# The end of a fused decode layer: the last addition as an fp32 product, the output by halves from partitions 0 and 1

## Chip, cores and metric

One core of a Trainium2 chip. The metric is the device time of one execution in microseconds, median over runs on the chip; the profile is one such execution, and its span (first to last instruction) is about 1.8 us shorter than the device time. The runs were made in several calls on different chips, so each kernel is compared with the kernel before in its own call.

The views name the engines PE (TensorE, the matrix products; PEld loads its weights), DVE (VectorE), ACT (ScalarE), POOL (GpSimd) and SP (SyncE); SPq and ACTq are the instructions with which SP and ACT issue transfers. The granted clock is the share of TensorE's full clock that the throttle allows.

## The reference

Attention of one new token (batch 2, 32 query heads over 16 key heads, the last 2048 keys of a bf16 cache) and a squared-ReLU MLP read the same normalised `x`; their outputs are added:

```python
xn = _layernorm(x, axis=-1)          # x: (2, 1, 576)
return x + _A_ref(xn, k, v, wq, wo) + _B_ref(xn, w1, b1, w2, b2)
# _B_ref: h = xn @ w1 + b1; r = max(h, 0); out = (r * r) @ w2 + b2   (w2: 4608 x 576)
```

The output is 2 x 576 bf16. Some 53.6 MB are loaded for it.

## The kernel before

Everything accumulates in PSUM. `out_ps` takes x, b2, the attention's output and three quarters of the MLP; it holds columns 0 to 287 in partitions 0 and 1 and columns 288 to 575 in partitions 32 and 33. The last quarter of w2 is loaded in two pieces (rows 0 to 6 and 7 to 8 of each partition) and accumulates in `tail_ps`, four quarters of 144 columns in four column groups, so that its few products run together:

```python
def mlp_tail(r0, r1):
    w2_sb = w2_tiles.pop((NG4 - 1, r0))
    if r0 == 0:
        mlp["out"] = psum.tile([P, OQ], F32, tag="misc", name="tail_ps")   # OQ = 144
        nc.vector.memset(mlp["out"][:], 0.0)
    for r in range(r0, r1):
        o = (r - r0) * D
        for i in range(4):
            pe_mm(mlp["out"][32 * i:32 * i + B, :], lhsT=mlp["h"][:, (NG4 - 1) * FR + r, :],
                  rhs=w2_sb[:, o + i * OQ:o + (i + 1) * OQ], start=(r == 0), stop=(r == FR - 1),
                  skip_group_check=True, tile_position=(0, 32 * i))
# ... (cut)
for w in W2P[:NG4 - 1]:
    mlp_o(*w)                                  # three quarters into out_ps
for i in range(4):                             # copy the rest to where tail_ps has it
    cp = nc.scalar.copy if i % 2 else nc.vector.tensor_copy
    cp(out=part[32 * i:32 * i + B, :],
       in_=out_ps[32 * (i // 2):32 * (i // 2) + B, (i % 2) * OQ:(i % 2 + 1) * OQ])
for w in W2P[NG4 - 1:]:
    mlp_tail(*w[1:])
fin_sb = work.tile([RB, OQ], BF16, tag="fin", name="fin_sb")               # RB = 98
nc.vector.tensor_tensor(out=fin_sb[:], in0=mlp["out"][0:RB, :], in1=part[:], op=ALU.add)
for b, eng in ((0, nc.sync), (1, nc.scalar)):  # one output row on each queue
    eng.dma_start(out=out2d[b:b + 1, :].rearrange("o (q n) -> (o q) n", q=4), in_=fin_sb[b:RB:32, :])
```

Of the kernel before, what the change touches and what calls it, by code (L numbers as in the profile page):

```python
# [8 lines left out]
F32 = mybir.dt.float32  # L9
BF16 = mybir.dt.bfloat16  # L10
ACT = mybir.ActivationFunctionType
ALU = mybir.AluOpType
# [4 lines left out]
def kernel(  # L17
# [14 lines left out]
    nc = tc.nc  # L32
    P = 128
    B, Sq, D = A_x.shape
# [30 lines left out]
    NG4 = 4  # L65
# [6 lines left out]
    RB = 32 * (NG4 - 1) + B  # L72
    OH = D // 2
    OQ = D // 4
# [3 lines left out]

    const = ctx.enter_context(tc.tile_pool(name="const", bufs=1))
    kvpool = ctx.enter_context(tc.tile_pool(name="kvpool", bufs=6))  # L80
    ktpool = ctx.enter_context(tc.tile_pool(name="ktpool", bufs=3))
    wbig = ctx.enter_context(tc.tile_pool(name="wbig", bufs=NFULL // RW))
    wrem = ctx.enter_context(tc.tile_pool(name="wrem", bufs=1))
    wopool = ctx.enter_context(tc.tile_pool(name="wopool", bufs=1))
    work = ctx.enter_context(tc.tile_pool(name="work", bufs=2))
# [3 lines left out]
    def pe_mm(out, **kw):  # L89
        return tc.keep_in_program_order(nc.tensor.matmul(out, **kw))  # L90
# [5 lines left out]
    out2d = out.rearrange("b s d -> (b s) d")  # L96
# [62 lines left out]
    nc.scalar.dma_start(out=x_sb[:], in_=x2d)  # L159
    eps_t = const.tile([B, 1], F32, name="eps_t")  # L160
    nc.vector.memset(eps_t[:], 1e-5)
    warm = const.tile([B, 34], F32, name="warm")
    nc.scalar.activation(out=warm[:, 0:1], in_=eps_t[:], func=ACT.Sqrt)
    for f in issue_kv(k_tiles, A_k_cache, 0, "k"):
        f()
# [14 lines left out]
    ident_f = const.tile([P, P], F32, name="ident_f")  # L180
# [27 lines left out]
    for sg in range(S):  # L208
# [8 lines left out]
                            op=ALU.add)  # L217
# [6 lines left out]
                            in0=ident[0:TH, 0:TH].unsqueeze(1).unsqueeze(3).to_broadcast([TH, P // NC, TH, rep]),  # L224
# [3 lines left out]
                          in_=ident[0:TH, 0:TH].unsqueeze(1).to_broadcast([TH, NT * 32 // TH, TH]))  # L228
    par = const.tile([P, 2, 2, Dh // 2], BF16, name="par")
    for e in range(2):  # L230
        nc.gpsimd.tensor_copy(out=par[:, e, :, :],
                              in_=ident[:, e:Dh:2].unsqueeze(1).to_broadcast([P, 2, Dh // 2]))
# [7 lines left out]
    out_ps = psum.tile([32 + B, OH], F32, tag="out", name="out_ps")  # L240
    nc.vector.memset(out_ps[:], 0.0)

    def out_acc(lhsT, rhs_of, start=False, stop=False):
        for i in range(2):
            pe_mm(out_ps[32 * i:32 * i + B, :], lhsT=lhsT, rhs=rhs_of(i * OH, (i + 1) * OH),
                  start=start, stop=stop, skip_group_check=True)
# [152 lines left out]
    mlp = {}  # L399
# [30 lines left out]
    def mlp_o(g, r0, r1):  # L430
        w2_sb = w2_tiles.pop((g, r0))
        for r in range(r0, r1):
            o = (r - r0) * D
            out_acc(mlp["h"][:, g * FR + r, :], lambda a, z: w2_sb[:, o + a:o + z], stop=(g == NG4 - 2 and r == r1 - 1))

    part = const.tile([RB, OQ], F32, name="part")
    nc.gpsimd.memset(part[:], 0.0)

    def mlp_tail(r0, r1):
        w2_sb = w2_tiles.pop((NG4 - 1, r0))  # L440
        if r0 == 0:
            mlp["out"] = psum.tile([P, OQ], F32, tag="misc", name="tail_ps")
            nc.vector.memset(mlp["out"][:], 0.0)
        for r in range(r0, r1):
            o = (r - r0) * D
            for i in range(4):
# [3 lines that stand above are left out]
# [9 lines left out]
    W2P = [(0, 0, 9), (1, 0, 9), (2, 0, 9), (3, 0, 7), (3, 7, 9)]  # L459
# [36 lines left out]
    for w in range(2):  # L496
# [7 lines left out]
                          in_=ident[0:NG4, 0:NG4].unsqueeze(2).to_broadcast([NG4, NG4, 32]))  # L504
# [34 lines left out]
    wo_acc(1)  # L539
    for w in W2P[:NG4 - 1]:  # L540
        mlp_o(*w)
    for i in range(4):
        cp = nc.scalar.copy if i % 2 else nc.vector.tensor_copy
        cp(out=part[32 * i:32 * i + B, :],  # L544
           in_=out_ps[32 * (i // 2):32 * (i // 2) + B, (i % 2) * OQ:(i % 2 + 1) * OQ])
    for w in W2P[NG4 - 1:]:
        mlp_tail(*w[1:])

    fin_sb = work.tile([RB, OQ], BF16, tag="fin", name="fin_sb")
    nc.vector.tensor_tensor(out=fin_sb[:], in0=mlp["out"][0:RB, :], in1=part[:], op=ALU.add)  # L550
    for b, eng in ((0, nc.sync), (1, nc.scalar)):
        eng.dma_start(out=out2d[b:b + 1, :].rearrange("o (q n) -> (o q) n", q=4), in_=fin_sb[b:RB:32, :])


# [28 lines left out]
```

## Time and profile before

| | before |
|---|---|
| device time, median of 6 (range) | 134.69 us (134.63 to 134.99) |
| span of the profiled run | 132.7 us |
| queue of the loads | 53.61 MB, 95.0% of the span |
| last landing of w2 to the end | 3.55 us |

The prediction shows the lines behind this table. Loads run from the first slices to 129.2 us without a gap. Whatever is done before that is hidden; only the 3.55 us after the last landing can be shortened or lengthened by this change, unless it disturbs the loads (the prediction's rival D).

### The profile page before, as it was taken

Reading aid. Unit: us, or ns where it says so; the run is one execution under the profiler, and the core shown is the slowest. Engines: PE = TensorE matmul, PEld = TensorE weight load, DVE = VectorE, ACT = ScalarE, POOL = GpSimd, SP = SyncE. Lnnn points to the kernel's source line nnn. Section 1 sums busy time; section 2 is a strip of 40 time slices with the busy share of each in tenths; the row PEclk is TensorE's granted clock in tenths of the full one; section 3 lists DMA queues with packets and bytes.
Section 4 is the critical chain, followed back from the end, with each engine's and each line's share of the span. In section 5 each row is a group of like instructions: output and inputs, shape, how many; then the busy total and the mean of one; then the engine's idle time right before and its main releaser. Section 6 shows DMA issues by size and latency. Waiting matters only on the chain.

```text
span 132.7 us, 2060 instructions
## 1 busy us (share of the span) xinstructions
PE 92.7 (70%) x838; PEld 55.9 (42%) x838; DVE 61.2 (46%) x169; ACT 46.3 (35%) x63; POOL 7.5 (6%) x21
## 2 busy tenths in 40 slices
PE   0069456897499689688787629959937985556960
PEld 0058222673456355444444325524515942313640
DVE  6914304346533872863764772287041436443010
ACT  5717301494343274175175043412040661000010
POOL 7500000100100100100100100010000001000000
PEclk9999977779769999999999995995995599655896
DMA  4999999999999999999999999999999999999940
GB/s 159 396 412 449 415 444 415 439 420 430 437 420 444 415 449 415 439 425 434 425 415 449 420 435 433 427 433 444 417 425 430 430 434 439 406 425 434 414 203 1
DMA packets 4268, 53.74 MB, mean 405 GB/s; under 512 B 542, under 2 KB 544, under 8 KB 1060
## 3 DMA queue, kind: packets, MB, share of 16 engines
q1 hardware_dynamic: 4184, 53.61, 95.0%
q8 instruction: 6, 0.10, 0.3%
q0 software_dynamic: 64, 0.01, 0.0%
q14 instruction: 2, 0.02, 0.0%
q10 hardware_dynamic: 12, 0.00, 0.0%
HBM read 53.62 MB, written 0.00 MB: 404 GB/s over the span
## 4 chain that ended last, share of the span: by engine, by line
DMA 88%; PE 7%; SPq 3%; issue 0%; DVE 0%; DVEq 0%
DMA k<-in_A_k_cache_dram 67%; DMA w<-in_B_w_dram 21%; PE kT_ps L93 4%; SPq L111 1%; PE pv_ps L90 1%; SPq L118 1%; PE sc_ps L90 1%; SPq L123 0%; PE tail_ps L90 0%; DVE fin_sb L550 0%; PE sm L90 0%; DVEq L550 0%
## 5 line engine op out<-in xcount | busy, mean ns | idle before, releaser
L93 PE MATMUL kT_ps<-ident_f,k 128*128 128x128 f32 x256 | 43.7, 322 | 6.6 <-DMA k<-in_A_k_cache_dram 4.9
L297 ACT COPY kT<-kT_ps 128x1024 bf16<-128x1024 bf16 x32 | 31.8, 1012 | 30.1 <-PE kT_ps L93 30.1
L93 PEld LDWEIGHTS kT_ps<-ident_f,k 128*128 128x128 f32 x256 | 34.3, 165 | 18.6 <-issue 6.6
L299 DVE COPY kT<-kT_ps 128x1024 bf16<-128x1024 bf16 x32 | 22.0, 686 | 29.9 <-PE kT_ps L93 29.1
L90 PE MATMUL sc_ps<-kT,qz 128*32 128x512 bf16 x128 | 9.7, 383 | 6.2 <-DVE kT L299 5.5
L90 PE MATMUL pv_ps<-v,pT 128*32 128x512 bf16 x128 | 13.5, 467 | 0.0
L330 ACT ACTIVATE pr<-sc_ps,nb 128x512 bf16<-128x512 f32 x8 | 5.5, 687 | 20.7 <-DVE nb L327 20.7
L323 POOL PARTITION_ALL_REDUCE gmax<-m x8 | 2.9, 364 | 102.7 <-DVE m L321 80.4
L368 DVE SCALAR_TENSOR_TENSOR acc<-pv_ps,f,acc 128x128 f32<-128x128 f32 x24 | 8.3, 346 | 0.5
L90 PE MATMUL sm<-acc,tohead 128*64 128x128 f32 x16 | 4.2, 352 | 5.8 <-DVE acc L368 5.5
L332 DVE STREAM_TRANSPOSE pT<-pr 128x512 bf16<-128x512 bf16 x8 | 5.7, 709 | 5.2 <-ACT pr L330 5.2
L90 PE MATMUL out_ps<-wo,ws 128*2 128x288 bf16 x64 | 6.7, 390 | 1.1 <-DVE ws L390 1.1
L319 DVE TENSOR_REDUCE mx<-sc_ps 128x1 f32<-128x512 f32 x8 | 5.5, 692 | 3.4 <-PE sc_ps L90 3.0
L90 PEld LDWEIGHTS <-qz 128*32 128x32 bf16 x128 | 2.0, 94 | 10.0 <-DVE kT L299 7.1
L544 ACT COPY part<-out_ps 2x144 f32<-2x144 f32 x2 | 0.5, 268 | 15.0 <-DVE part L544 14.9
L90 PEld LDWEIGHTS <-ws 128*2 128x2 bf16 x64 | 3.7, 114 | 4.6 <-DVE ws L390 1.5
L90 PE MATMUL sm<-sums,samec 128*128 128x1 f32 x16 | 3.3, 276 | 3.1 <-DVE od L386 3.1
L90 PEld LDWEIGHTS sm<-acc,tohead 128*64 128x64 f32 x16 | 1.8, 161 | 8.6 <-DVE acc L368 7.9
L90 PEld LDWEIGHTS <-xnT 128*2 128x2 bf16 x100 | 2.6, 87 | 6.7 <-issue 5.5
L90 PEld LDWEIGHTS <-pT 128*32 128x32 bf16 x128 | 3.3, 102 | 4.3 <-issue 4.0
L90 PE MATMUL q_ps<-wq,xnT 128*2 128x512 bf16 x32 | 2.9, 499 | 3.2 <-DMA wq<-in_A_wq_dram 3.2
L93 PE MATMUL pro_ps<-ident,xn_sb 2*128 2x2 bf16 x4 | 0.3, 172 | 6.7 <-DVE xn_sb L198 6.7
(86 smaller groups left out, 62.3 us busy)
## 6 DMA issues: line engine op xcount, KB each, us to landing
k<-in_A_k_cache_dram SPq DMA_DIRECT2D x8, 2048.0 KB, 22.0
v<-in_A_v_cache_dram SPq DMA_DIRECT2D x8, 2048.0 KB, 27.0
wo<-in_A_wo_dram SPq DMA_DIRECT2D x2, 2304.0 KB, 23.4
w<-in_B_w_dram SPq DMA_DIRECT2D x2, 2304.0 KB, 30.9
wq<-in_A_wq_dram SPq DMA_DIRECT2D x2, 2048.0 KB, 13.9
w<-in_B_w_dram SPq DMA_DIRECT2D x3, 1296.0 KB, 27.7
w<-in_B_w_dram SPq DMA_DIRECT2D x1, 1008.0 KB, 31.8
w_rem<-in_B_w_dram SPq DMA_DIRECT2D x1, 576.0 KB, 34.2
```

The lines of the kernel that those rows point to most:

```text
L90: return tc.keep_in_program_order(nc.tensor.matmul(out, **kw))
L93: return tc.keep_in_program_order(nc.tensor.transpose(**kw))
L111: return [lambda i=i: nc.sync.dma_start(out=tl[:, i * n:(i + 1) * n], in_=v[:, :, i * n:(i + 1) * n]) for i in range(parts)]
L118: nc.sync.dma_start(out=tl[:, 0:RW * width], in_=rows[:, i * RW * width:(i + 1) * RW * width])
L297: nc.scalar.copy(out=dst, in_=src)
L299: nc.vector.tensor_copy(out=dst, in_=src)
L319: nc.vector.tensor_reduce(out=mx[:], in_=sc_ps, axis=AX.X, op=ALU.max)
L323: nc.gpsimd.partition_all_reduce(gmax[:], m2[:], channels=P, reduce_op=ReduceOp.max)
L330: nc.scalar.activation(out=pr[:], in_=sc_ps, func=ACT.Exp, bias=nb[:], scale=scale, accum_out=sums[:])
L332: nc.vector.transpose(out=pT[:].rearrange("p t m -> p (t m)"), in_=pr[:])
L368: op = nc.vector.scalar_tensor_tensor(out=nx[:], in0=pv_ps[:, j, :], scalar=f[:, j:j + 1], in1=acc[:], op0=ALU.mult, op1=ALU.add)
L544: cp(out=part[32 * i:32 * i + B, :], in_=out_ps[32 * (i // 2):32 * (i // 2) + B, (i % 2) * OQ:(i % 2 + 1) * OQ])
```

## The change

Its intent: add the rest not by a DVE addition over 98 partitions, but inside the accumulators, by a product with an identity; then the accumulators are copied to two partitions and leave as two halves of 576 B a row. Core of the diff:

```diff
-    ktpool = ctx.enter_context(tc.tile_pool(name="ktpool", bufs=3))
+    ktpool = ctx.enter_context(tc.tile_pool(name="ktpool", bufs=2))
-    warm = const.tile([B, 34], F32, name="warm")
+    warm = const.tile([B, 114], F32, name="warm")
-    part = const.tile([RB, OQ], F32, name="part")      # and its memset, and that of tail_ps
+    part = const.tile([B, D], F32, name="part")
 ...
-    for i in range(4):                                 # four copies to four quarters
-        ...
-    for w in W2P[NG4 - 1:]:
-        mlp_tail(*w[1:])
+    for i in range(2):
+        nc.vector.tensor_copy(out=part[:, i * OH:(i + 1) * OH], in_=out_ps[32 * i:32 * i + B, :])
+    mlp_tail(*W2P[NG4 - 1][1:])
+    for i in range(4):
+        pe_mm(mlp["out"][32 * i:32 * i + B, :], lhsT=ident_f[0:B, 0:B], rhs=part[:, i * OQ:(i + 1) * OQ],
+              start=False, stop=False, skip_group_check=True, tile_position=(0, 32 * i))
+    mlp_tail(*W2P[NG4][1:])
-    nc.vector.tensor_tensor(out=fin_sb[:], in0=mlp["out"][0:RB, :], in1=part[:], op=ALU.add)
-    for b, eng in ((0, nc.sync), (1, nc.scalar)):
-        eng.dma_start(out=out2d[b:b + 1, :].rearrange("o (q n) -> (o q) n", q=4), in_=fin_sb[b:RB:32, :])
+    for i, (cp, eng) in enumerate(((nc.vector.tensor_copy, nc.sync), (nc.scalar.copy, nc.scalar))):
+        fin_sb = work.tile([B, OH], BF16, tag="fin", name=f"fin_sb_{i}")
+        for q in range(2):
+            k = 2 * i + q
+            cp(out=fin_sb[:, q * OQ:(q + 1) * OQ], in_=mlp["out"][32 * k:32 * k + B, :])
+        eng.dma_start(out=out2d[:, i * OH:(i + 1) * OH], in_=fin_sb[:])
```

More of the change, by code (lines that the diff above doesn't have):

```diff
@@ L434, in mlp_o @@
             out_acc(mlp["h"][:, g * FR + r, :], lambda a, z: w2_sb[:, o + a:o + z], stop=(g == NG4 - 2 and r == r1 - 1))
-    part = const.tile([RB, OQ], F32, name="part")
-    nc.gpsimd.memset(part[:], 0.0)
+    part = const.tile([B, D], F32, name="part")
     def mlp_tail(r0, r1):
@@ L442, in mlp_tail @@
             mlp["out"] = psum.tile([P, OQ], F32, tag="misc", name="tail_ps")
-            nc.vector.memset(mlp["out"][:], 0.0)
         for r in range(r0, r1):
@@ L541 @@
         mlp_o(*w)
+    for i in range(2):
+        nc.vector.tensor_copy(out=part[:, i * OH:(i + 1) * OH], in_=out_ps[32 * i:32 * i + B, :])
+    mlp_tail(*W2P[NG4 - 1][1:])
     for i in range(4):
-        cp = nc.scalar.copy if i % 2 else nc.vector.tensor_copy
-        cp(out=part[32 * i:32 * i + B, :],
-           in_=out_ps[32 * (i // 2):32 * (i // 2) + B, (i % 2) * OQ:(i % 2 + 1) * OQ])
-    for w in W2P[NG4 - 1:]:
-        mlp_tail(*w[1:])
-    fin_sb = work.tile([RB, OQ], BF16, tag="fin", name="fin_sb")
-    nc.vector.tensor_tensor(out=fin_sb[:], in0=mlp["out"][0:RB, :], in1=part[:], op=ALU.add)
-    for b, eng in ((0, nc.sync), (1, nc.scalar)):
-        eng.dma_start(out=out2d[b:b + 1, :].rearrange("o (q n) -> (o q) n", q=4), in_=fin_sb[b:RB:32, :])
+        pe_mm(mlp["out"][32 * i:32 * i + B, :], lhsT=ident_f[0:B, 0:B], rhs=part[:, i * OQ:(i + 1) * OQ],
[7 more added lines that the diff above has]
+        eng.dma_start(out=out2d[:, i * OH:(i + 1) * OH], in_=fin_sb[:])
 _INS = ['A_x', 'A_k_cache', 'A_v_cache', 'A_wq', 'A_wo', 'B_x', 'B_w1', 'B_b1', 'B_w2', 'B_b2']
```

## The prediction

> **What bounds the kernel now.** I read the page first (engines' shares, the 40 slices, queues, the chain that ended last), then the chain piece by piece, then the timeline of the last microseconds. From the page:
>
> ```profile
> DMA  4999999999999999999999999999999999999940
> q1 hardware_dynamic: 4184, 53.61, 95.0%
> DMA 88%; PE 7%; SPq 3%; issue 0%; DVE 0%; DVEq 0%
> DMA k<-in_A_k_cache_dram 67%; DMA w<-in_B_w_dram 21%; PE kT_ps L93 4%; SPq L111 1%; PE pv_ps L90 1%; SPq L118 1%; PE sc_ps L90 1%; SPq L123 0%; PE tail_ps L90 0%; DVE fin_sb L550 0%; PE sm L90 0%; DVEq L550 0%
> ```
>
> The DMA row is full from the second slice to the next to last, and one queue moves 53.61 MB in 95% of the span of 132.7 us. So the loads set the time, and compute counts only after the last load has landed. The pieces of the chain at its end (start, length, what):
>
> ```profile
> 101.64 27.55 DMA w<-in_B_w_dram
> ...
> 129.23 0.32 PE tail_ps L90 x8
> ...
> 129.65 0.31 DVE fin_sb L550
> ```
>
> The last rows of w2 land at 129.19. Eight products take 0.32 us, a semaphore some 0.1, the DVE addition 0.31, and from 129.98 the output transfers run to the end, 2.72 us for issue, write and closing. The diff touches this tail almost alone. Its timeline:
>
> ```profile
> 127.66 0.63 DVE L544 COPY part<-out_ps 2x144 f32<-2x144 f32 x2 [7.07 <-PE out_ps L90]
> 128.04 0.56 ACT L544 COPY part<-out_ps 2x144 f32<-2x144 f32 x2 [14.94 <-DVE part L544]
> ...
> 128.52 1.00 PE L90 MATMUL tail_ps<-w,hT_sb 128*2 128x144 bf16 x36 [0.90 <-DMA w<-in_B_w_dram]
> ...
> 129.65 0.31 DVE L550 TENSOR_TENSOR fin_sb<-tail_ps,part 98x144 bf16<-98x144 f32 x1 [1.36 <-PE tail_ps L90]
> 129.98 0.66 SPq L552 DMA_DIRECT2D out_dram<-fin_sb  x1
> ```
>
> Two loads end the stream: rows 0 to 6 of the last w2 quarter (1008 KB) release TensorE at 128.52, rows 7 and 8 (288 KB) at 129.23, 0.71 us later. Narrower cuts of the timeline show that the 28 products of the first load started between 128.52 and 128.90 in groups of four, about 0.06 us apart (0.38 us over 27 gaps is 14 ns each), so TensorE has free time only from about 128.96 to 129.23: **0.27 us**.
>
> **What the skill says.** (1) FP8 and Floating Point Precision, section TensorE Precision Notes: true fp32 takes four passes through the array. The trace agrees in the one fp32 product of this shape: eight calls gave 16 instructions, and two of them started about 0.13 us apart at full clock for 128 columns (0.40 us for both less 0.27 for one), close to two passes of 128 columns each.
>
> ```profile
> 46.24 0.40 PE L90 MATMUL sm<-acc,tohead 128*64 128x128 f32 x2 [0.41 <-DVE acc L368]
> 32.78 0.28 PE L90 MATMUL out_ps<-x_sb,ident 2*2 2x288 bf16 x2
> ```
>
> (2) TensorE: Matmul & The Clock Gate, Part 3, "What overlaps and what doesn't": products start and end in program order, while those in different column groups may run at once. The trace agrees: 14 ns from start to start in the tail is a quarter of the 0.06 us of one group, and the two products of the second line above took 0.28 us together, as long as one alone (median 0.278). (3) TensorEngine Tiling (Array Packing), Key Properties: a change of tiling mode drains the array. The trace is compatible: the last score product ahead of that second line started at 32.48; products of that row follow each other in one group after about 0.23 us (32.24 to 32.47), yet the 2-row products came at 32.78, about 0.07 to 0.09 us later than that. (4) DMA: Bandwidth & Descriptors, Specifications: under 512 B a transfer pays a read-modify-write. The output now goes as four pieces of 288 B per queue and would go as two of 576 B. The trace does not show such a cost by itself: the write lies inside the 2.72 us.
>
> **The change part by part.**
>
> *Removed, no gain.* The GpSimd memset of `part` (0.22 us at 1.6 us) and the DVE memset of `tail_ps` (0.18 us at 118.9) lie beside other work. Both go, worth 0.
>
> *Two instead of three kT tiles.* Each half unit of K fills one tile. When the copies for the first half of unit u+1 want a buffer again, its reader, the first scores of unit u, stands ahead of unit u+1's transposes on the in-order TensorE, and the copies wait for these anyway. The same holds for the second half. No new wait: 0. I take the smaller pool to be room for the wider `part`, which goes from 576 to 2304 B per partition; with `warm` (136 to 456 B) the constants grow by 1728 + 320 = 2048 B, so the big load tiles keep their position modulo 2 KiB. I expect the rate of about 430 GB/s in the middle slices to stay.
>
> *Copies of the rest.* Two DVE copies of 2x288 replace four of 2x144. A 2x144 copy takes 0.298 us; at about 1.04 ns a column (the DVE copies of 128x512 fp32 in the transposed-reduction row take 0.69 us, which gives about the same slope) a 2x288 one takes about 0.45. From 127.66 that ends near 128.6. The fp32 products come no earlier than 128.96, so there are 0.35 us in hand: 0.
>
> *The fp32 products.* Four calls are eight instructions of two passes of 144 columns each: 288 columns at the measured 0.06 us per 144 give 0.12 us an instruction. The two halves of one call use one column group, so the second starts 0.12 after the first. Only the first half of the next call can start with it, because of program order. The starts are at 0, .12, .12, .24, .24, .36, .36 and .48, with the end of streaming at 0.60. Beginning at 128.96 without any drain, the last eight bf16 products then end about 0.35 us later than now (final group start 129.64 against 129.29). If the change from 128-row to 2-row operands and back drains the array, 0.08 to 0.09 us is added twice: 0.53. I take **+0.44**. The free 0.27 us is already deducted in both.
>
> *The end.* One DVE addition of 0.31 us becomes two DVE copies of 2x144 one behind the other. The like pair at 127.66 took 0.63, so **+0.32**. ACT's pair took 0.56 and runs beside it: at line 544 an ACT copy of one quarter (128.04) ran during a DVE copy of another (127.98), and here the engines read different quarters of the partitions again. The DVE pair and the SP queue's issue (0.66 against ACT's 0.61) set the end.
>
> *Output.* Same two issues, half the pieces, each twice as long: **-0.05**, a guess about a part that the trace does not separate.
>
> Sum: 0.44 + 0.32 - 0.05 = +0.71 us. On 134.68 that is 135.39; I put down 135.35, because the later launch of work might also hide a little.
>
> **Rivals.**
>
> *A: the fp32 products are hidden.* If their passes interleave over the four groups, they need some 0.24 us and fit the 0.27 us nearly whole. Against it: the instructions of one call stand together and start in order. The sum would be +0.16 or less for TensorE, about 135.0 in all.
>
> *B: they run one after another.* If fp32 takes the whole array, eight times 0.12 is 0.96 us, which with drains makes TensorE's part about +0.9 and the time 135.9. The bf16 2-row pair at 32.78 that ran together speaks against it, but no fp32 product in column groups is in this trace.
>
> *C: the output write becomes cheaper than I think,* as the diff's intent seems to be (rows of 576 B from partitions 0 and 1). If the 288 B pieces cost a few tenths, the end gives back 0.2 to 0.4 and the time is about 135.0. With A it would be near 134.7, no change.
>
> *D: the moved buffers alter the load stream.* Every load tile changes its address. One per cent of DMA rate is 1.3 us, more than all the rest together. For it: the loads are the bound. Against it: the padding keeps the alignment, and order, sizes and queue of the loads stay.
>
> *E: ACT waits for DVE at the end,* if the reads of the shared accumulator are put in order: ACT's pair would end 0.56 us later still, 135.9. The overlap at line 544 speaks against it.
>
> **Range and chances.** A and C give the lower part, B and E the upper; D widens both sides. I take 134.75 to 135.9. Two per cent is 2.7 us, far beyond any sum of these terms, so the chance of "within 2%" is 0.97, with 0.01 for faster and 0.02 for slower (D or a stall that I don't see).
>
> **What would show it right or wrong.** In the changed profile the DMA row and the landing of the last w2 rows should stay within about 0.3 us of 129.2. TensorE should have 846 products instead of 838. The last `tail_ps` products should end some 0.35 to 0.55 us after where they end now (129.53), not 0.1 (A) nor 0.9 (B). Two DVE copies of about 0.3 us each should stand in a row ahead of the SP issue, with ACT's beside them. From SP's issue to the end there should be 2.6 to 2.75 us; clearly less is C. If the last load lands much earlier or later, D holds and my sum says nothing about the time. Last, no copy of kT should wait longer than before for a buffer.

## The result, and the profile after

| | before | after |
|---|---|---|
| device time, median of 6 (range) | 134.69 us (134.63 to 134.99) | 134.51 us (134.37 to 134.59) |
| ratio | | 0.998 (95%: 0.9967 to 0.9993) |
| span of the profiled run | 132.7 us | 132.7 us |

A ratio is the mean time of one kernel's runs over that of the other's of the same rounds, so not quite the ratio of the medians quoted. The result lies within 2%, as forecast, but below the stated range of 134.75 to 135.9, on the other side of "before".

The page of the kernel after: the loads are as they were.

```profile
DMA  4999999999999999999999999999999999999950
q1 hardware_dynamic: 4180, 53.61, 95.1%
```

The timeline of its tail (start, length, engine, what, count, and in brackets the idle time before it with what ended it):

```profile
127.50 0.93 DVE L541 COPY part<-out_ps 2x288 f32<-2x288 f32 x2 [8.86 <-PE out_ps L90]
...
128.64 0.61 PE L90 MATMUL tail_ps<-w,hT_sb 128*2 128x144 bf16 x28 [1.17 <-DMA w<-in_B_w_dram]
...
129.17 0.42 PE L90 MATMUL tail_ps<-part,ident_f 2*2 2x144 f32 x8
...
129.53 0.29 PE L90 MATMUL tail_ps<-w,hT_sb 128*2 128x144 bf16 x8
129.85 0.63 DVE L552 CAST fin_sb<-tail_ps 2x144 bf16<-2x144 f32 x2 [1.42 <-PE tail_ps L90]
129.92 0.57 ACT L552 CAST fin_sb<-tail_ps 2x144 bf16<-2x144 f32 x2 [17.45 <-PE tail_ps L90]
130.50 0.33 SPq L553 DMA_DIRECT2D out_dram<-fin_sb  x1
```

The eight fp32 instructions are there, the two pairs of copies run side by side, and the issue at the end takes 0.33 us where it took 0.66. To add this up, both tails are put on one zero: the last landing of w2, which the trace's semaphore records give. Output packets are from the trace's packet records. All in us after that landing:

| kernel, clock in the tail | landing at | last 8 products start | their end | copies or addition start | SP issue starts | first SP output packet | end |
|---|---|---|---|---|---|---|---|
| before, full | 129.19 | 0.04 | 0.34 | 0.46 | 0.80 | 2.15 | 3.55 |
| after, full | 129.30 | 0.22 | 0.52 | 0.55 | 1.20 | 2.00 | 3.42 |

Step by step: the fp32 products delay the last eight by 0.18; the gap from the products' end to the first DVE instruction shrinks from 0.12 to 0.03 (-0.09; the addition had a further wait instruction ahead of it, probably since it needed `part` as well); two copies in place of one addition take 0.32 longer; from issue to end there are 2.22 us in place of 2.76 (-0.54; the prediction's 2.72 came from the rounded span). The sum is -0.13, close to the -0.18 of the medians. That the two spans are equal to a tenth is because the loads of this one profile landed 0.12 us later (over all twenty profiles the last landing lies between 129.11 and 129.48).

### The profile page after: what moved, and what is told of

The parts are those of the page before. It is cut to its first block, busy times and chain, and to the rows that moved or that the text cites. A ratio compares the mean times of both kernels' runs of the same rounds, so it can differ in the third digit from the quotient of the medians.

```text
span 132.7 us, 2075 instructions
## 1 busy us (share of the span) xinstructions
PE 90.6 (68%) x846; PEld 54.2 (41%) x846; DVE 61.5 (46%) x169; ACT 46.2 (35%) x63; POOL 7.3 (6%) x20
## 4 chain that ended last, share of the span: by engine, by line
DMA 73%; PE 13%; SPq 4%; DVE 3%; issue 2%; ACT 2%; POOL 1%; ACTq 0%; POOLq 0%
DMA w_rem<-in_B_w_dram 26%; DMA w<-in_B_w_dram 24%; DMA k<-in_A_k_cache_dram 23%; PE kT_ps L93 8%; PE pv_ps L90 2%; PE sc_ps L90 2%; SPq L118 1%; ACT kT L297 1%; SPq L111 1%; DVE kT L299 1%; DVE mx L319 1%; PE tail_ps L90 1%; POOL gmax L323 1%; SPq L142 0%; SPq L123 0%
## 5 line engine op out<-in xcount | busy, mean ns | idle before, releaser
L93 PEld LDWEIGHTS kT_ps<-ident_f,k 128*128 128x128 f32 x256 | 33.4, 163 | 20.2 <-issue 7.6
L90 PE MATMUL sc_ps<-kT,qz 128*32 128x512 bf16 x128 | 10.5, 413 | 6.5 <-DVE kT L299 5.5
L90 PE MATMUL pv_ps<-v,pT 128*32 128x512 bf16 x128 | 12.4, 428 | 0.0
L90 PE MATMUL sm<-acc,tohead 128*64 128x128 f32 x16 | 3.7, 315 | 5.7 <-DVE acc L368 5.5
L319 DVE TENSOR_REDUCE mx<-sc_ps 128x1 f32<-128x512 f32 x8 | 5.5, 691 | 4.2 <-PE sc_ps L90 3.8
L90 PE MATMUL out_ps<-wo,ws 128*2 128x288 bf16 x64 | 5.9, 356 | 1.1 <-DVE ws L390 1.1
L552 ACT CAST fin_sb<-tail_ps 2x144 bf16<-2x144 f32 x2 | 0.5, 272 | 17.5 <-PE tail_ps L90 17.4
L541 DVE COPY part<-out_ps 2x288 f32<-2x288 f32 x2 | 0.9, 448 | 8.9 <-PE out_ps L90 8.9
```

Source lines behind the costliest of these rows:

```text
L90: return tc.keep_in_program_order(nc.tensor.matmul(out, **kw))
L93: return tc.keep_in_program_order(nc.tensor.transpose(**kw))
L319: nc.vector.tensor_reduce(out=mx[:], in_=sc_ps, axis=AX.X, op=ALU.max)
L541: nc.vector.tensor_copy(out=part[:, i * OH:(i + 1) * OH], in_=out_ps[32 * i:32 * i + B, :])
```

## The experiments

### What in the output transfer cost: pieces, their size, or the source

The largest miss is the output, so it came first. The output leaves in pieces, each one row of the source tile that is contiguous on both sides. Theory P says that issue and set-up grow with the number of pieces, theory Z that pieces under 512 B are slow, theory S that a source is slow which takes every 32nd partition. The first two kernels change only the pieces, by a gap in the SBUF tile:

```diff
-        fin_sb = work.tile([B, OH], BF16, ...)
+        fin_sb = work.tile([B, 2, OQ + 16], BF16, ...)
-            cp(out=fin_sb[:, q * OQ:(q + 1) * OQ], ...)
+            cp(out=fin_sb[:, q, 0:OQ], ...)
-        eng.dma_start(out=out2d[:, i * OH:(i + 1) * OH], in_=fin_sb[:])
+        eng.dma_start(out=out2d[:, i * OH:(i + 1) * OH].rearrange("b (q n) -> b q n", q=2), in_=fin_sb[:, :, 0:OQ])
```

(Four pieces of 288 B; the second kernel does the same with four gaps of 72 columns, eight pieces of 144 B.)

> The changed kernel, but each output transfer goes as four pieces of 288 B (two partitions, two pieces each, kept apart by a gap in the SBUF tile) in place of two of 576 B. Theory P (issue and set-up grow with the number of pieces): SP issue back to 0.6 to 0.66 us, from issue start to first output packet about 1.35 us as before the change, time 0.4 to 0.55 us above the changed kernel, so 0.25 to 0.35 above the kernel before. Theory S (it was the step of 32 partitions at the source that cost): issue 0.33, time as the changed kernel. Theory Z (pieces under 512 B are written slower): issue 0.33, but packets or landing later by 0.1 to 0.5 us.

> As the run with four pieces, but eight of 144 B per transfer. P: SP issue 1.2 to 1.3 us, first packet some 2.4 us after issue start, time about 1.5 us above the changed kernel. S: as the changed kernel. Z: issue 0.33 us, landing later.

Measured: 135.05 us (134.4 to 135.34; before 134.87; ratio to before 1.0005, 0.9985 to 1.0024) and 134.76 us (ratio 0.9983, 0.9971 to 0.9996). The output's instructions with four pieces, with shortest, median and longest duration in ns:

```profile
L553 SPq DMA_DIRECT2D out_dram<-fin_sb x1: 327/327/327, 131.3 to 131.3; - x1
```

With eight pieces SP's issue took 326 ns. The first SP packet came 0.75 us after the start of the issue in both. So theory P is refuted. From the end of the last output packet to the last landing it took 0.44 and 0.43 us (after: 0.46), so theory Z is refuted as well. The longer times of the four-piece kernel have another cause, at least in its profiled run, treated below: the tail ran at half clock.

The third kernel goes the other way, one piece of 1152 B on each queue:

```diff
-        eng.dma_start(out=out2d[:, i * OH:(i + 1) * OH], in_=fin_sb[:])
+    for b, eng in ((0, nc.sync), (1, nc.scalar)):        # one tile [2, 576] written by DVE and ACT
+        eng.dma_start(out=out2d[b:b + 1, :], in_=fin_sb[b:b + 1, :])
```

> The changed kernel with one output tile: SP sends row 0, ACT row 1, each one piece of 1152 B, each after both engines' copies. P: SP issue 0.17 to 0.2 us, first packet 0.5 to 0.6 us after issue start, time 0.1 to 0.25 us below the changed kernel. S and Z: issue 0.33, time as the changed kernel or up to 0.05 above (ACT waits for DVE).

Measured: 134.85 us (134.48 to 135.3), ratio 1.0001 (0.9981 to 1.002); the profile, at full clock, has an issue of 312 ns, the first packet 0.80 us after it and 3.43 us from landing to end, as after the change. Again theory P fails.

The fourth takes the kernel before and halves each transfer, keeping the partitions 32 apart:

```diff
-        eng.dma_start(out=out2d[b:b + 1, :].rearrange("o (q n) -> (o q) n", q=4), in_=fin_sb[b:RB:32, :])
+    for h in range(2): ...
+            eng.dma_start(out=out2d[b:b + 1, h * OH:(h + 1) * OH].rearrange("o (q n) -> (o q) n", q=2),
+                          in_=fin_sb[64 * h + b:64 * h + b + 33:32, :])
```

> The kernel before, with its two output transfers of four pieces cut into four of two pieces each (288 B, source partitions 32 apart), two on each queue. P: each issue 0.3 to 0.35 us, the second of a queue ends where the one of before ended, time within 0.1 us of before. S: each issue still about 0.6 us, time 0.5 to 0.6 us above before. If a fixed cost per issue dominates: also above, by 0.2 to 0.3.

Measured: 135.73 us, ratio 1.0063 (1.0051 to 1.0075). Two pieces cost as much as four did:

```profile
L553 SPq DMA_DIRECT2D out_dram<-fin_sb x2: 638/642/646, 130.4 to 131.1; - x2
```

This is S, with a larger total than S had said (0.86 in place of 0.5 to 0.6 us above before): the second issue starts 0.69 us after the first, and its first packet comes 1.55 us after that. Some 0.27 us of the profiled run (135.92 us) are the clock: its tail ran at half clock, and the addition started 0.73 us after the landing in place of 0.46. Next, the kernel before with eight transfers of a single partition, so no steps at all:

> The kernel before with its output in eight transfers of one partition each (288 B, one piece, four on each queue), so that no transfer steps over partitions. If the step of 32 partitions in one transfer costs (theory S): each issue 0.31 us like the single piece of 1152 B, four in a row end 0.6 us later than the one of before, time 0.3 to 0.7 us above before. If any source outside the first 32 partitions costs: issue 0.31 for quarter 0, 0.6 for the others, time 1.3 us or more above before.

Measured: 135.24 us, ratio 1.004 (1.0028 to 1.0052), about 0.53 us above before, as S said. The issues from partitions 0, 32, 64 and 96 all are short:

```profile
L553 SPq DMA_DIRECT2D out_dram<-fin_sb x4: 248/282/312, 130.1 to 131.1; - x4
```

x1 to x4 were to tell what it is in a stepping source that costs. All are the kernel before with one transfer of two pieces of 288 B on each queue (half of the output is never written). Only source and target differ:

```diff
+ x1: out2d[b:b + 1, 0:OH] as two rows, in_=fin_sb[0:2, :]            # step 1, adjacent targets
+ x2: out2d[:, b * OQ:(b + 1) * OQ],    in_=fin_sb[b:b + 33:32, :]    # step 32
+ x3: out2d[:, b * OQ:(b + 1) * OQ],    in_=fin_sb[b:b + 3:2, :]      # step 2
+ x4: out2d[:, b * OQ:(b + 1) * OQ],    in_=fin_sb[32:34, :]          # step 1, other quarter
```

> The kernel before, but each queue sends two pieces of 288 B from partitions 0 and 1 to adjacent places of one output row (wrong result on purpose, as in the next three: half of the output is not written). If the source step costs: SP issue 0.33 us, first packet 0.75 to 0.8 us after issue start. If adjacent rows at the target cost: 0.64 and 1.3 or more.

> Two pieces from partitions 0 and 32 (SP) or 1 and 33 (ACT) to the two output rows, 1152 B apart. Source step costs: issue 0.64 us, first packet 1.3 us or more. Target's adjacency costs: 0.33 and 0.8.

> Two pieces from partitions 0 and 2 (SP) or 1 and 3 (ACT) to the two output rows. If any step over partitions above one costs: as the step of 32, 0.64 and 1.3. If it takes another quarter of the partitions: 0.33 and 0.8.

> Two pieces from partitions 32 and 33 to the two output rows. Step theory: 0.33 and 0.8. If the place beyond the first 32 partitions costs: 0.64 and 1.3 (the single pieces from 32, 64 and 96 speak against it).

SP's line of the timeline in these four, in this order:

```profile
130.07 0.34 SPq L552 DMA_DIRECT2D out_dram<-fin_sb  x1
```

```profile
130.19 0.64 SPq L552 DMA_DIRECT2D out_dram<-fin_sb  x1
```

```profile
130.15 0.74 SPq L552 DMA_DIRECT2D out_dram<-fin_sb  x1
```

```profile
130.18 0.34 SPq L552 DMA_DIRECT2D out_dram<-fin_sb  x1
```

From issue start to the first SP packet: 0.78, 1.24, 1.34 and 0.77 us. From issue start to the end of the span: 2.19, 2.83, 2.84 and 2.18 us. So it is the step: two neighbouring partitions anywhere are cheap, two partitions with a step of 2 or 32 between them are not, and neither the target's layout nor the place matters. Each is one run, but the two kinds lie far apart. Why a step costs, no run shows.

### The fp32 products

In the first of these the products are left out (the result is wrong); in the second they open the accumulation instead of standing between the two loads' rows:

```diff
+    mlp["out"] = psum.tile([P, OQ], F32, tag="misc", name="tail_ps")
+    for i in range(4):
+        pe_mm(mlp["out"][32 * i:32 * i + B, :], lhsT=ident_f[0:B, 0:B], rhs=part[:, i * OQ:(i + 1) * OQ],
+              start=True, ...)
     mlp_tail(*W2P[NG4 - 1][1:])       # its first rows now with start=False
-    for i in range(4): ...            # the products that stood here
     mlp_tail(*W2P[NG4][1:])
```

The unchanged kernel ran beside them.

> The changed kernel unchanged, as the base for the two that follow. If the tail falls on the full clock: last eight products start about 0.22 us after the last landing, time 0.1 to 0.25 us below the kernel before. If the granted clock drops to 0.5 in the tail (as in the profile of the run with four pieces, whose products took some 0.5 us longer): up to 0.7 us longer, so some of the runs near 135.2.

> The changed kernel without the four fp32 products (wrong result on purpose: the rest is missing). If they cost what the two traces say (0.18 us at full clock): last eight products start 0.04 us after the last landing, time 0.18 us below the changed kernel; at half clock 0.6 to 0.7 below. If they were hidden after all (rival A): same time as the changed kernel.

> The changed kernel with the fp32 products ahead of the first rows of the last w2 quarter (they open the accumulation), in the 1.1 us in which TensorE waits for that load. If what costs is their place between the two loads' products: they begin about 128.5, the last eight start 0.04 to 0.08 us after the last landing, time as without products, 0.15 to 0.2 below the changed kernel at full clock, and the spread to longer times shrinks. If they then push the first rows back: up to 0.1 less gain.

| run, clock in its profile | times of all runs | last 8 start after landing | end after landing |
|---|---|---|---|
| changed kernel, second time, half | 134.38 to 134.6, and 135.36 | 0.86 | 4.16 |
| without products, full | 134.15 to 134.32 | 0.04 | 3.23 |
| products first, full | 134.26 to 134.91 | 0.04 | 3.21 |

Before: 134.71; the changed kernel's second series has the ratio 0.9992 (0.9972 to 1.0011). At full clock the products where the change puts them cost 0.18 to 0.21 us (0.22 - 0.04, and 3.42 less 3.23 or 3.21), and in these profiles all of it comes from their place. The timeline with the products first shows them in the waits for the two DVE copies:

```profile
127.48 0.92 DVE L539 COPY part<-out_ps 2x288 f32<-2x288 f32 x2 [7.16 <-PE out_ps L90]
...
127.98 0.89 PE L90 MATMUL tail_ps<-part,ident_f 2*2 2x144 f32 x8 [0.53 <-DVE part L539]
...
128.80 0.60 PEld L90 LDWEIGHTS <-hT_sb 128*2 128x2 bf16 x36 [0.25 <-issue]
128.80 0.79 PE L90 MATMUL tail_ps<-w,hT_sb 128*2 128x144 bf16 x36
```

But some runs were longer, and so the gain is not in the mean: ratio 0.9986 (0.9971 to 1.0), where the expectation had the spread shrink. Without the products it is 0.9964 (0.9951 to 0.9977).

### The long runs: the granted clock

The profile of the second series of the changed kernel fell on its long run, 135.36 us:

```profile
128.71 1.01 PE L90 MATMUL tail_ps<-w,hT_sb 128*2 128x144 bf16 x28 [1.16 <-DMA w<-in_B_w_dram]
...
129.65 0.66 PE L90 MATMUL tail_ps<-part,ident_f 2*2 2x144 f32 x8
...
130.24 0.41 PE L90 MATMUL tail_ps<-w,hT_sb 128*2 128x144 bf16 x8
```

Every stage of TensorE took longer than in the short run (0.61, 0.42 and 0.29), and the end came 0.74 us later after the landing. The Trainium skill (TensorE: Matmul & The Clock Gate, Part 1, "What's actually happening") says that the clock is halved or restored by free-running windows of about 3.4 us, by how busy the array was. The clock records of these profiles agree: only 1.0 and 0.5 occur, in stretches of about 3.4 us and its multiples. Theory C of the experiments (not the prediction's rival C): the run is long when a window with little TensorE work ends just ahead of the tail. The test adds products without use in the gap after the last `out_ps` product, two ahead of early fp32 products and three in the otherwise unchanged kernel:

```diff
+    keep_ps = psum.tile([P, 512], F32, tag="sc", bufs=2, name="keep_ps")
+    # after the last mlp_o, two (products first) or three times (changed kernel):
+    pe_mm(keep_ps[:], lhsT=ident[:], rhs=qz[:, 0, :, :, :, :].rearrange("p u w j c -> p (u w j c)"),
+          start=True, stop=True, skip_group_check=True)
```

> The run with the products first once more, as the base for the next. Runs with the tail at full clock near 134.3, others 0.3 to 0.6 us longer.

> Products first, and two products of 512 columns without use in the gap after the last out_ps product, to keep TensorE busy there. If the long runs come from the granted clock falling in the tail after a window with little work (theory C): no run above 134.5, median 134.25 to 134.35. If the long runs have another cause, they stay; if the added products stand in the way, all runs are 0.1 to 0.4 us longer.

> The changed kernel with three such products of 512 columns in the same gap, otherwise unchanged. Theory C: no run near 135.3, all 134.35 to 134.6. Otherwise one or two of six near 135.2 as in the runs of the changed kernel.

Measured: products first again 134.23 to 135.22, ratio 1.0 (0.998 to 1.0021); products first and busy 134.41 to 134.76, median 134.68, ratio 0.9996 (0.9984 to 1.0008), where theory C forecast 134.25 to 134.35; changed kernel and busy 134.34 to 134.59, median 134.41 against 134.70 before, ratio 0.9984 (0.9972 to 0.9996). The profiles of the long run above and of the last happen to have the same clock windows up to 128.7. Stretches of both (length, busy time and count of PE and of its weight loads, DVE, ACT, POOL, granted clock, DMA share, GB/s), first the long run:

```profile
125.30:128.70 3.40, 1.27 (x18) 0.70 (x17) 0.89 (x2) 0.00 (x0) 0.00 (x0) 1.00 0.74 307
128.70:131.30 2.60, 1.94 (x44) 0.90 (x44) 0.59 (x2) 0.54 (x2) 0.00 (x0) 0.50 0.02 6
```

```profile
125.30:128.70 3.40, 2.05 (x25) 0.95 (x28) 0.90 (x2) 0.00 (x0) 0.00 (x0) 1.00 0.72 298
128.70:131.30 2.60, 1.16 (x44) 0.58 (x44) 0.59 (x2) 0.55 (x2) 0.00 (x0) 1.00 0.01 5
```

With 1.27 us of work in the window the clock fell, with 2.05 it stayed. The other profiles agree. The four-piece kernel and the kernel before with halved transfers had 1.30 and 1.27 us in the window up to 128.7, and the clock fell; the result's profile had 1.59 us up to 128.96, and it stayed, as in all others, whose last window ahead of or in the tail held 1.8 us or more. That supports the theory but gives no limit: elsewhere windows with more work were followed by half clock (products first, 126.73 to 130.14, 2.26 us). The five timed runs without a long one add little: of the changed kernel's own 17 runs only one was long. The kernel before is exposed too, but less: half clock delayed its addition by 0.27 us (above), and the changed kernel's copies by 0.74 (1.29 after the landing in place of 0.55).

In the profile of products first and busy the last eight started 0.35 us after the landing in place of 0.04, but the added products are not what delayed them:

```profile
127.60 0.61 PE L90 MATMUL keep_ps<-qz,ident 128*128 128x512 bf16 x2
127.70 0.93 DVE L547 COPY part<-out_ps 2x288 f32<-2x288 f32 x2 [7.12 <-PE out_ps L90]
...
128.20 0.89 PE L90 MATMUL tail_ps<-part,ident_f 2*2 2x144 f32 x8
```

The fp32 products start 0.50 us after the first copy, as without the filling (127.98 after 127.48). The copies came 0.22 us later, because the last `out_ps` product, which stands ahead of the added ones, started at 127.38 in place of 127.16; and the last w2 rows landed 0.15 us earlier. A narrower filling, products of 2 rows, was tried last, with the changed kernel a third time beside it:

```diff
+    keep_clock(8)     # bf16, lhsT=ident[0:B, 0:B], rhs=khead[0:B, :] (512 columns), four column groups
     ...                                                       # the copies of part
+        if i == 2: keep_clock(4)                              # between the fp32 products
```

> Products first, and TensorE kept busy by products of 2 rows by 512 columns in four column groups (eight before the fp32 products, four between their halves), which are in the same tiling as these and should fit the waits for the two DVE copies. If such narrow products count as work for the clock (theory C) and don't delay: all runs 134.2 to 134.4, last eight products 0.05 us after the last landing. If narrow products don't keep the clock up: spread to 134.9 or 135.2 as without them. If they delay: all 0.1 to 0.2 longer.

> The changed kernel unchanged, third time: median 134.4 to 134.6, with none to two of six runs 0.5 to 0.9 us longer.

Measured: 134.8 us (134.31 to 135.21), ratio 1.0003, a miss; and 134.6 us (134.54 to 134.7), ratio 0.9986 (0.9974 to 0.9999). In the profile of the first the last eight started 0.43 us after the landing. Again the fp32 products follow the first copy by 0.50 us (128.36 after 127.86), and the copies are late. So with products first all 36 tail products stand behind the two copies, without slack (in the first such profile the products of the first load had all started only at 129.18, and the last load landed at 129.25), and a late end of `out_ps` goes straight into the end. That may be why these runs spread; none of their long runs was profiled. In four of the six runs, besides, the device time exceeds the span by 1.95 to 2.36 us, in all other runs by 1.74 to 1.87; that part lies outside the kernel's span, and its cause is not known. The second's profile shows one more effect. There the half clock had lain ahead of the tail (114.6 to 124.8), the last `out_ps` products ended later, and so the copies of the rest:

```profile
128.38 0.93 DVE L541 COPY part<-out_ps 2x288 f32<-2x288 f32 x2 [7.33 <-PE out_ps L90]
...
129.15 0.61 PE L90 MATMUL tail_ps<-part,ident_f 2*2 2x144 f32 x8
...
129.69 0.30 PE L90 MATMUL tail_ps<-w,hT_sb 128*2 128x144 bf16 x8
```

The second copy ended at 129.30, and the records have the second four of the eight fp32 instructions start only at 129.36. The last eight came 0.41 us after the landing, end 3.61.

What stays open: how often a run is long. Of the changed kernel's 17 runs one was, while of 17 runs with four, eight or one piece, whose TensorE work is the same, seven were above 134.9 (four, none and three; they ran on another chip, where before took 134.87).

### The moved buffers

```diff
-    ktpool = ctx.enter_context(tc.tile_pool(name="ktpool", bufs=3))
+    ktpool = ctx.enter_context(tc.tile_pool(name="ktpool", bufs=2))
-    warm = const.tile([B, 34], F32, name="warm")
+    warm = const.tile([B, 114], F32, name="warm")
-    part = const.tile([RB, OQ], F32, name="part")
+    part_t = const.tile([RB, D], F32, name="part"); part = part_t[:, 0:OQ]
```

> The kernel before with two kT tiles and with the constants grown as in the change (all load tiles 2 KiB further on), nothing else. If the tail explains the result: same as before within 0.1 us, no new wait of the kT copies, last landing 129.1 to 129.35 in the profile. If the moved buffers had changed the load stream (rival D) and helped: 0.2 us or more below before.

Measured: 134.82 us (134.54 to 135.13) against 134.70, ratio 1.0016 (1.0003 to 1.0029). The last landing was at 129.2 and the end 3.55 us after it, both as before. The copies of kT waited for the transposes alone. The move gains nothing. The interval lies just above 1, so it may cost up to 0.4 us; the profile, of the fastest of the five runs, shows no such cost, and the cause of the longer ones is open.

## Why the prediction was wrong

It put +0.71 us on the tail by its terms, and the measured sum is -0.13.

- **Output, -0.05: this step failed.** It treated the transfer as "same two issues, half the pieces, each twice as long" and called it a guess. The measured term is -0.54. It is neither number nor size of the pieces (four, eight and one behave as two do), but the step over partitions of the source: 0.64 to 0.74 us of issue and 1.24 us or more to the first packet with a step, 0.25 to 0.34 and 0.75 to 0.80 without one. The trace of before held a hint, no more: an issue of 0.66 us for 1.1 KB, as long as the longest issue of a 2 MB load (0.43 to 0.66). Rival C saw a gain here of 0.2 to 0.4, for a reason (rows of 576 B) that the runs refute; and by the prediction's own working A with C lay near 134.7, below its stated range.
- **fp32 products, +0.44: this step failed too; 0.18 at full clock.** The ladder of starts 0.12 us apart "because of program order" did not happen: the eight instructions started from 129.173 to 129.315, in two groups of four, 0.12 apart. The third series shows what the groups are. There only two of the four calls had their data at first, and their four instructions started in two pairs (129.154 and 129.161, 129.276 and 129.282). So the halves of one call do follow each other by 0.12 us, but in the profile of the result the first halves of all four calls started before the second half of the first call. Gaps of the size of the assumed drains are there: from the end of streaming, estimated at 129.08 (last start 129.02 plus 0.06), to 129.17, and again about 0.09 before 129.53; that they are drains is not shown. Rival A had the interleaving right, but not that the products are hidden.
- **End copies, +0.32: right** (0.626 against 0.308). Left out was a wait: the addition started 0.12 us after its products, a copy starts 0.03 after, -0.09.
- **Copies of the rest, 0: right in the profile of the result** (446 and 449 ns against 450 forecast, done 0.7 us ahead of the products), but not in each run: in the third series they came onto the path. What the prediction calls copies of 128x512 fp32 are, in the trace, reductions (L319, 0.69 us); the slope was still right.
- **Two kT tiles and memsets, 0: right.** No wait for a kT buffer is new. ACT's kT copies after the change stood idle for the transposes alone, as before (first line):

```profile
L297 ACT COPY kT<-kT_ps 128x1024 bf16<-128x1024 bf16 x32 | 31.8, 1012 | 30.1 <-PE kT_ps L93 30.1
L297 ACT COPY kT<-kT_ps 128x1024 bf16<-128x1024 bf16 x32 | 31.8, 1012 | 31.7 <-PE kT_ps L93 31.6
```

- **Load stream: right.** The last landing moved from 129.19 to 129.30, within the 0.3 allowed, and TensorE has 846 products. Nothing speaks for rival D as a gain. B does not appear: even at half clock the eight started in two groups of four, 0.19 us apart, though all of TensorE's delay there, 0.86 - 0.04 us, is of the size that B gave. E does not appear: ACT's copies run beside DVE's.

Of the miss of 0.84 us (0.71 forecast, -0.13 measured), 0.49 is the output, 0.26 the products and 0.09 the wait. The range left no room for two terms that err in the same direction.

No correct version clearly beats the changed kernel. Its form with a busy TensorE (134.41 against 134.70 before) had five short runs, but the first and the third series of the changed kernel itself were all short too.

## What to carry to other kernels

Where only the tail counts, an output transfer is not a constant: look at its issue duration and at the first packet, and gather the result in neighbouring partitions if the source steps. An extra pair of copies (0.32 us) was cheaper than such a step (0.54 us). Side products in a wait of TensorE, ahead of the last loads' products, saved 0.2 us in profiles in which their inputs were ready in time, and nothing in the mean of the runs: look at how much slack the inputs have. And know which clock window the tail met before you judge a difference of a few tenths.

## What the Trainium skill lacked or had wrong

- DMA: Bandwidth & Descriptors has, as far as I found, no cost for a transfer whose SBUF source steps over partitions by more than one. Here: issue 0.64 to 0.74 us against 0.34 for the same two pieces, first packet 1.24 to 1.34 us against 0.77 to 0.78 after issue start (SP queue).
- The same page, Specifications, states a read-modify-write for less than 512 B. At this size no run shows a penalty: with pieces of 144, 288, 576 and 1152 B the last landing came 0.43, 0.44, 0.46 and 0.45 us after the end of the last packet.
- FP8 and Floating Point Precision, TensorE Precision Notes, has the four passes of an fp32 product, but no page says how the instructions of fp32 calls in different column groups overlap. Here, by the trace's records, eight instructions of four calls started within 0.14 us, first halves before second halves; so the program order of starts, which the prediction took from TensorE: Matmul & The Clock Gate, Part 3, did not hold for them.
- TensorE: Matmul & The Clock Gate puts the penalty of the cold start under 1% of a typical span. Half clock in the tail cost 0.7 us of 134.5 here, which is within that but several times the effect of the whole change.
